# A gated linear recurrence ahead of a top-1 expert layer: every attention product 128 columns wide, and the copies, squares and limiter in another order

## The chip, the cores and the metric

The kernel runs on one core of a Trainium2 chip. The metric is the device time of one execution in microseconds (us). Five engines matter: TensorE (PE, matrix products; its weight loads are PEld), VectorE (DVE), ScalarE (ACT), GpSimd (POOL) and SyncE (SP, which issues the DMAs). Each works through its own queue in order.

## The reference

Attention is a recurrence with a complex gate per channel; the real part of its state answers the query. An expert layer follows: each token goes to the expert with its largest logit.

```python
mag = np.sqrt(a_re * a_re + a_im * a_im)
scale = np.minimum(mag, 0.999) / (mag + 1e-06)
a_re_n, a_im_n = (a_re * scale, a_im * scale)
for t in range(S):
    new_re = ar * S_re - ai * S_im
    new_im = ar * S_im + ai * S_re
    kv = np.einsum('bhd,bhe->bhde', k[:, :, t], v[:, :, t])
    S_re, S_im = (new_re + kv, new_im)
    y[:, :, t] = np.einsum('bhd,bhde->bhe', q[:, :, t], S_re)
...
expert_idx = np.argmax(logits, axis=1)
...
    h = np.maximum(xe @ w1[e], 0.0)
    ye = h @ w2[e]
    out[mask] = gate_w[mask, None] * ye
```

Sizes: batch 4, 8 heads, 768 tokens, 48 channels a head (384 in all); 8 experts with 1024 hidden units; all in 32-bit floats.

## The kernel before

The kernel has three parts: attention, routing, experts. Only attention is touched by the change.

**Preparation, per batch, on VectorE and ScalarE (`limit`, `front`).** The channels lie on partitions, in 3 tiles of 128; the 768 tokens of a batch are 6 chunks of 128 tokens, each in 8 blocks of 16 steps. `limit` works on a quarter of the steps at a time (four pieces): ScalarE squares the gates (`sq`), VectorE adds the squares (`s`), ScalarE takes logarithm, exponential and a square (`l`, `u`), VectorE and ScalarE make the scale (`sc`). `front` scales the gates of a batch (`X<-raw`, four operations), issues the loads of the next batch's gates (`raw`) and of this batch's `q` and `k` (`qt`, `kt_in`), and multiplies the gates up over 15 steps (`z`, `X<-z`). Between these steps it calls the pieces of the next batch's limiter. Then it carries the products over blocks (`carry`, `zc`). Per tile of 128 channels, `fix` applies the carry and `fold` multiplies the products into `q` and their inverse into `k` (`pk`), and sends both by DMA to the heads' tiles `KX` and `QX` (a ring of six each).

**Products (`attention`).** Heads go in three groups (2, 3 and 3 heads). For each chunk TensorE makes the scores (`at`, 224 columns: 128 of scores and 96 that move the state on), VectorE masks them (`am`), ScalarE copies the other 96 columns to `kt`. Then come the output (`y` from masked scores and values, and from the state `st`) and the next state (`sp`, copied to `st` by ScalarE); each of these products has 48 columns, one head's values. ScalarE copies `y` to `xf`. In the last group each chunk is also transposed (`px`, copied to `xt`) and multiplied with the gate weights to logits (`lg`); VectorE copies a batch's logits to `lg_all`.

**Order.** VectorE, ScalarE and TensorE run in the order in which the code is written (`InOrder`). `front` is a generator that yields estimated VectorE microseconds; `attention` is one that yields estimated TensorE microseconds. `heads_until` interleaves them: a piece of attention is emitted when the sum of VectorE estimates (`spent[0]`) has passed the sum of its own (`spent[1]`). A group is put in line 4 us (`SHIP`) after the fold that completes its heads. So a mask stands in VectorE's queue where the estimates put it; if TensorE lags, VectorE stops there, with the next batch's preparation behind.

SyncE issues all of this part's DMAs from one queue. A tile with several buffers (`bufs`) lets a load go out while earlier contents are still read; otherwise the load waits at the head of SyncE's queue, and the `KX` and `QX` copies wait behind it.

## Time and profile before

| | |
|---|---|
| median of three runs | 971.62 us (952.6 to 973.02) |
| profiled execution | 963.26 us, of it 961.5 us from first to last instruction |
| mean granted clock of TensorE | 0.806 |
| TensorE busy | 718.4 us (75%), weight loads 624.0 us |
| VectorE busy | 421.7 us (44%) |
| ScalarE busy | 208.3 us (22%) |

Busy shares are means over parts with different limits: attention ends at 566.6 us, routing at about 600, and the experts take the rest. They are best read by stretches. The granted clock is given as a share of 2.4 GHz; it has two levels, 0.50 (1.2 GHz) and 1.00 (2.4 GHz), so a value between is a mean over time. In the trace a 32-bit product is two records (`x2`). The start of one instruction to the start of the next on TensorE tells its pace; the length of a record also holds the time through the array.

### The profile page before, as it was taken

How to read it: one execution, taken by the hardware profiler on the slowest of the kernel's cores; microseconds unless marked ns; L12 is line 12 of the kernel's file. 1: busy time of each engine (PE TensorE's matmuls, PEld its weight loads, DVE VectorE, ACT ScalarE, POOL GpSimd, SP SyncE). 2: the span in 40 equal slices, each digit the busy share in tenths (PEclk: the TensorE clock that was granted, in tenths of full speed). 3: DMA queues.
4: the chain of work that ended last, by engine and by line, in shares of the span. 5: the costliest groups of instructions: out<-in, count | busy, mean ns of one | idle time of the engine just before them, and what ended most of it. 6: DMA issues, size and time to landing. Idle time of an engine off the chain costs nothing. (4 is left out here: it accounts for less than half of the span.)

```text
span 961.5 us, 10708 instructions
## 1 busy us (share of the span) xinstructions
PE 718.4 (75%) x3985; PEld 624.0 (65%) x3985; DVE 421.7 (44%) x764; ACT 208.3 (22%) x486; POOL 138.0 (14%) x160
## 2 busy tenths in 40 slices
PE   0000578893967947998499951999999999999997
PEld 0000578783967846987499840777777777777775
DVE  3779966549657568854952015111111111111111
ACT  5442343322344123322232110000000000000000
POOL 6000000000000000000000002133333333333320
PEclk9999985555577557875569555999999999999999
DMA  7301471124270134412431003878797779878860
GB/s 213 99 0 49 113 177 62 44 57 124 53 212 18 49 89 117 124 51 61 120 72 37 26 19 102 355 313 311 296 361 295 301 296 395 313 308 316 326 232 1
DMA packets 67627, 156.47 MB, mean 163 GB/s; under 512 B 9873, under 2 KB 50866, under 8 KB 59634
## 3 DMA queue, kind: packets, MB, share of 16 engines
q0 software_dynamic: 12896, 108.36, 29.3%
q1 hardware_dynamic: 51474, 47.36, 18.7%
q8 instruction: 33, 0.54, 0.2%
q10 hardware_dynamic: 3200, 0.01, 0.2%
q14 instruction: 24, 0.20, 0.1%
HBM read 127.23 MB, written 10.83 MB: 144 GB/s over the span
## 5 line engine op out<-in xcount | busy, mean ns | idle before, releaser
L57 PE MATMUL at<-QX,KX 128*128 128x224 f32 (+1 forms) x384 | 124.7, 485 | 153.6 <-DVE QX L57 137.4
L57 PEld LDWEIGHTS at<-QX,KX 128*128 128x128 f32 x384 | 95.4, 277 | 160.4 <-issue 104.4
L675 PEld LDWEIGHTS h_ps<-xt,w1t 128*128 128x128 f32 x1488 | 173.2, 194 | 13.2 <-issue 5.3
L675 PE MATMUL h_ps<-xt,w1t 128*128 128x128 f32 x1488 | 173.4, 277 | 4.9 <-issue 4.9
L681 PE MATMUL o_ps<-w2t,ht 128*128 128x384 f32 x496 | 167.8, 492 | 8.5 <-ACT ht L677 8.2
L681 PEld LDWEIGHTS o_ps<-w2t,ht 128*128 128x128 f32 x496 | 91.7, 190 | 71.7 <-ACT ht L677 14.1
L57 PE MATMUL y<-vb,am 128*128 128x48 f32 x384 | 90.6, 336 | 17.8 <-DVE am L57 15.8
L57 PEld LDWEIGHTS y<-vb,am 128*128 128x128 f32 x384 | 86.4, 270 | 21.2 <-issue 17.1
L677 ACT ACTIVATE ht<-h_ps 128x512 f32<-128x512 f32 x31 | 18.5, 597 | 357.3 <-PE h_ps L675 357.3
L57 PE MATMUL y<-st,QX 128*128 128x48 f32 x320 | 85.1, 358 | 3.0 <-ACT st L57 2.9
L683 DVE TENSOR_SCALAR yo<-o_ps,xs 128x384 f32<-128x384 f32 x31 | 19.1, 618 | 143.8 <-PE o_ps L681 143.8
L57 DVE TENSOR_TENSOR am<-at,causal 128x256 f32<-128x256 f32 x120 | 41.3, 366 | 93.1 <-ACT kt L57 70.1
L445 POOL MEMSET state<- 128x1152 f32 x1 | 1.1, 1062 | 550.1 <-PE lg L57 550.1
L670 DVE COPY xt<-xt_ps 128x384 f32<-128x384 f32 x31 | 17.3, 557 | 139.9 <-PE xt_ps L668 139.8
L57 PE MATMUL sp<-vb,kt 128*128 128x48 f32 x320 | 74.9, 334 | 0.0
L57 PEld LDWEIGHTS y<-st,QX 128*128 128x128 f32 x320 | 71.3, 275 | 4.4 <-ACT st L57 3.9
L57 PE MATMUL sp<-st,QX 128*128 128x48 f32 x256 | 64.6, 343 | 0.0
L57 PEld LDWEIGHTS sp<-vb,kt 128*128 128x128 f32 x320 | 63.5, 252 | 0.0
L684 POOL DMA_INDIRECT out_dram<-yo,idx x31 | 31.5, 1016 | 194.8 <-DVE yo L683 193.9
L57 PEld LDWEIGHTS sp<-st,QX 128*128 128x128 f32 x256 | 54.2, 261 | 0.0
L57 DVE SCALAR_TENSOR_TENSOR s<-sq 128x576 f32<-128x576 f32 (+1 forms) x28 | 23.6, 842 | 65.9 <-ACT sq L57 65.9
L57 PEld LDWEIGHTS lg<-wgate,xt 128*128 128x128 f32 x144 | 29.4, 297 | 30.0 <-ACT xt L57 30.0
(142 smaller groups left out, 757.4 us busy)
## 6 DMA issues: line engine op xcount, KB each, us to landing
KX<-pk SPq DMA_DIRECT2D x48, 146.2 KB, 3.4
QX<-pk SPq DMA_DIRECT2D x48, 144.0 KB, 3.5
raw<-in_a_re_dram SPq DMA_DIRECT2D x16, 288.0 KB, 4.9
raw<-in_a_im_dram SPq DMA_DIRECT2D x16, 288.0 KB, 5.4
qt<-in_q_dram SPq DMA_DIRECT2D x12, 384.0 KB, 5.8
kt_in<-in_k_dram SPq DMA_DIRECT2D x12, 384.0 KB, 5.8
vb<-in_v_dram SPq DMA_DIRECT2D x24, 192.0 KB, 3.0
x_hbm<-xf SPq DMA_DIRECT2D x24, 192.0 KB, 2.7
```

The lines of the kernel that those rows point to most:

```text
L57: return lambda *a, **kw: self.tc.keep_in_program_order(f(*a, **kw))
L445: nc.gpsimd.memset(state, 0.0)
L670: nc.vector.tensor_copy(xt, xt_ps)
L675: nc.tensor.matmul(h_ps[:, f, :], lhsT=w1t[:, c:c + 128], rhs=xt[:, d, :], start=(d == 0), stop=(d == DT - 1))
L677: nc.scalar.activation(ht[:, 0:FT // 2, :], h_ps[:, 0:FT // 2, :], func=ACT.Relu)
L681: nc.tensor.matmul(o_ps, lhsT=ht[:, f, :], rhs=w2t[:, f * DM:f * DM + DM], start=(f == 0), stop=(f == FT - 1))
L683: nc.vector.tensor_scalar_mul(y, o_ps, xs[:, DM:W])
L684: nc.gpsimd.indirect_dma_start(out=out[:, :], out_offset=bass.IndirectOffsetOnAxis(ap=idx[:, j:j + 1], axis=0), in_=y, in_offset=None, bou ...
```

## The change

- Every `y` and `sp` product takes 128 columns of the values: the head's own 48 and its neighbours' (`first`, `own`). PSUM tiles `y`, `sp` and the state `st` are 128 wide per head; the copy to `xf` picks the head's 48 columns, in one instruction for the first two groups and in three for the last.
- The mask of chunk c+1 is emitted ahead of the outputs of chunk c. The copies out of PSUM are emitted after the estimate for their products, and `kt` is copied after the mask.
- The logits of a chunk are emitted after the next chunk's outputs, and ScalarE instead of VectorE copies a batch's logits.
- In `limit` the squares of a piece are issued one piece ahead, into a double buffer; the order of the stages within a piece changes. In `front` the limiter is called only from step 7 on, twice a step.
- The set-up tiles of the masks lie in a pool that is freed, and `qt` and `kt_in` have one buffer instead of two.
- The estimates in the yields change.

```diff
--- before.py
+++ after.py
@@ -87,31 +87,32 @@
-    tok_i = consts.tile([128, 128], I32, name="tok_i")
...
+    with tc.tile_pool(name="setup", bufs=1) as setup:
+        tok_i = setup.tile([128, 128], I32, name="tok_i")
+        nc.gpsimd.iota(tok_i, pattern=[[1, BL], [BL, NB]], base=0, channel_multiplier=0)
...
@@ -164,12 +165,18 @@
 
         def limit(b, raws, scales):
 
-            held = {}
+            held, sqs = {}, {}
+
+            def squares(i):
+                if i < BL // JQ:
+                    sq = two.tile([128, BL, 2, C * NB], FP32, name="sq").rearrange("p j u n -> p (j u n)")[:, 0:JQ * 2 * NC]
+                    sqs[i] = sq.rearrange("p (j u n) -> p j u n", u=2, n=NC)
+                    A.activation(sqs[i], raws[i], func=ACT.Square)
+            squares(0)
             for i in range(BL // JQ + 2):
                 if i < BL // JQ:
-                    sq = one.tile([128, JQ, 2, NC], FP32, name="sq")
-                    A.activation(sq, raws[i], func=ACT.Square)
                     s = two.tile([128, JQ, NC], FP32, name="s")
+                    sq = sqs.pop(i)
                     vstt(s, sq[:, :, 0, :], 1e-12, sq[:, :, 1, :], ALU.max, ALU.add)
                     yield
                 if i >= 2:
@@ -178,14 +185,6 @@
                     sc = two.tile([128, JQ, NC], FP32, name="sc", bufs=BL // JQ)
                     vstt(sc, l, -2 / 0.999, u, ALU.max, ALU.mult)
                     scales.append(sc)
-                    yield
-                if 1 <= i <= BL // JQ:
-
-                    s1, l, u = held[i - 1]
-                    vtt(s1, s1, u, ALU.mult)
-                    yield
-                    vstt(l, s1, -3.0, l, ALU.add, ALU.mult)
-                    A.activation(u, l, func=ACT.Identity, scale=-0.5e-6 * 0.4995, bias=w_bias)
                     yield
                 if i < BL // JQ:
                     l, u = (two.tile([128, JQ, NC], FP32, name=x) for x in "lu")
@@ -193,6 +192,15 @@
                     A.activation(l, l, func=ACT.Exp, scale=-0.5)
                     A.activation(u, l, func=ACT.Square, accum_out=good[:, b, G * C + i:G * C + i + 1])
                     held[i] = s, l, u
+                    squares(i + 1)
+                if 1 <= i <= BL // JQ:
+
+                    s1, l, u = held[i - 1]
+                    vtt(s1, s1, u, ALU.mult)
+                    yield
+                    vstt(l, s1, -3.0, l, ALU.add, ALU.mult)
+                    A.activation(u, l, func=ACT.Identity, scale=-0.5e-6 * 0.4995, bias=w_bias)
+                    yield
 
         def front(b, raws, scales, heads, ahead):
 
@@ -206,18 +214,19 @@
             qs, ks = [], []
             for t in range(G):
                 for x, src in ((qs, q), (ks, k)):
-                    x.append(ld.tile([128, BL, C * NB], FP32, name="qt" if x is qs else "kt_in"))
+                    x.append(ld.tile([128, BL, C * NB], FP32, name="qt" if x is qs else "kt_in", bufs=1))
                     nc.sync.dma_start(x[t], src[b, :, t])
 
             for j in range(1, BL):
                 cur, prev = X[:, j], X[:, j - 1]
                 z = two.tile([128, 2, 2, NC], FP32, name="z")
                 vtt(z, dims(cur, 0, (NC, 2), (NC, 2), (1, NC)), dims(prev, 2 * NC, (-NC, 2), (0, 2), (1, NC)), ALU.mult)
-                next(more, None)
+                if j > 6:
+                    next(more, None)
                 vtt(cur[:, 1:3, :], z[:, 0], z[:, 1], ALU.add)
-                if j > 8:
+                if j > 6:
                     next(more, None)
-                yield 1.8
+                yield 2.4 if j > 6 else 1.3
             for _ in more:
                 pass
 
@@ -253,7 +262,7 @@
 
             def fold(t):
                 ts = slice(t * TC, t * TC + TC)
-                sq = one.tile([128, BL, 2, TC], FP32, name="sq")
+                sq = two.tile([128, BL, 2, TC], FP32, name="sq")
                 s, l = (two.tile([128, BL, TC], FP32, name=x) for x in "sl")
                 A.activation(sq, X[:, :, 1:3, ts], func=ACT.Square)
                 qp = two.tile([128, 2, KW], FP32, name="pk", bufs=3)
@@ -326,6 +335,10 @@
                 lgs[:] = [psL.tile([128, C, E], FP32, name="lg")]
             pairs = [range(p, min(p + 2, n)) for p in range(0, n, 2)]
 
+
+            first = [min(h * D, DM - 128) for h in hs]
+            own = [slice(h * D - f, h * D - f + D) for h, f in zip(hs, first)]
+
             def scores(c):
                 wide = 128 + (R2 if c < C - 1 else 0)
                 ats = []
@@ -334,17 +347,17 @@
                     for i in r:
                         T.matmul(at[:, i % 2, 0:wide], lhsT=KX[i][:, c * 128:c * 128 + 128], rhs=QX[i][:, c, 0:wide],
                                  start=True, stop=True)
-                    if c < C - 1:
-                        A.copy(KTs[c % 2][:, r[0]:r[-1] + 1, 0:R2], at[:, 0:len(r), 128:wide])
                     ats.append(at)
                 return ats
 
-            def masks(ats):
+            def masks(c, ats):
                 am = []
                 for r, at in zip(pairs, ats):
                     a = sm.tile([128, 2, 128], FP32, name="am", bufs=4)
                     vtt(a[:, 0:len(r), :], at[:, 0:len(r), 0:128], bc(causal[:, None, :], [128, len(r), 128]), ALU.mult)
                     am += [a[:, i % 2, :] for i in r]
+                    if c < C - 1:
+                        A.copy(KTs[c % 2][:, r[0]:r[-1] + 1, 0:R2], at[:, 0:len(r), 128:128 + R2])
                 spent[0] += 0.07 * len(pairs) + 0.134 * n
                 return am
 
@@ -354,47 +367,63 @@
                 vtt(QX[i][0:R2, 0:C - 1, 128:128 + R2].rearrange("p c (w d) -> p c w d", w=2),
                     bc(diag[:, None, :, :], shape), bc(ends, shape), ALU.mult)
                 spent[0] += 0.57
+            yield 0.6
             ats = scores(0)
-            yield 0.45 * n + 1.0
-            am = masks(ats)
-            st = None
+            yield 0.4 * n + 0.3
+            am = masks(0, ats)
+            st, late = None, None
+
+            def logits(c, xt):
+                for d in range(DT):
+                    T.matmul(lgs[0][:, c, :], lhsT=xt[:, d, :], rhs=wgate[:, d * E:d * E + E], start=(d == 0), stop=(d == DT - 1))
             for c in range(C):
                 if c < C - 1:
                     ats = scores(c + 1)
-                    yield 0.43 * n
-                y = psY.tile([128, 3, D], FP32, name="y")
+                    yield 0.38 * n
+                    am1 = masks(c + 1, ats)
+                y = psY.tile([128, 3, 128], FP32, name="y")
                 for i, h in enumerate(hs):
-                    T.matmul(y[:, i, :], lhsT=am[i], rhs=values[c][:, h, :], start=True, stop=(c == 0))
+                    vals = values[c].rearrange("p h e -> p (h e)")[:, first[i]:first[i] + 128]
+                    T.matmul(y[:, i, :], lhsT=am[i], rhs=vals, start=True, stop=(c == 0))
                     if c > 0:
                         T.matmul(y[:, i, :], lhsT=QX[i][:, c, 0:128], rhs=st[:, i, :], start=False, stop=True)
-                A.activation(xf[:, c, hs[0] * D:hs[-1] * D + D].rearrange("p (h e) -> p h e", e=D), y[:, 0:n, :],
-                             func=ACT.Copy, scale=-1.0)
-                yield 0.44 * n
+                if late:
+                    logits(*late)
+                    late = None
+                yield 0.46 * n
+                if own[0] == own[n - 1]:
+                    A.activation(xf[:, c, hs[0] * D:hs[-1] * D + D].rearrange("p (h e) -> p h e", e=D), y[:, 0:n, own[0]],
+                                 func=ACT.Copy, scale=-1.0)
+                else:
+                    for i, h in enumerate(hs):
+                        A.activation(xf[:, c, h * D:h * D + D], y[:, i, own[i]], func=ACT.Copy, scale=-1.0)
                 if c < C - 1:
-                    am = masks(ats)
-                    sp = psS.tile([128, 3, D], FP32, name="sp")
+                    sp = psS.tile([128, 3, 128], FP32, name="sp")
                     for i, h in enumerate(hs):
+                        vals = values[c].rearrange("p h e -> p (h e)")[:, first[i]:first[i] + 128]
                         if c > 0:
                             T.matmul(sp[:, i, :], lhsT=QX[i][:, c, 128:], rhs=st[:, i, :], start=True, stop=False)
-                        T.matmul(sp[:, i, :], lhsT=KTs[c % 2][:, i, :], rhs=values[c][:, h, :], start=(c == 0), stop=True)
-                    st = sm.tile([128, 3, D], FP32, name="st", bufs=2)
+                        T.matmul(sp[:, i, :], lhsT=KTs[c % 2][:, i, :], rhs=vals, start=(c == 0), stop=True)
+                    yield 0.46 * n
+                    st = sm.tile([128, 3, 128], FP32, name="st", bufs=2)
                     A.copy(st[:, 0:n, :], sp[:, 0:n, :])
-                    yield 0.44 * n
+                    am = am1
                 if g == G - 1:
                     px = psX.tile([128, DT, 128], FP32, name="px")
                     for d in range(DT):
                         T.transpose(px[:, d, :], xf[:, c, d * 128:d * 128 + 128], ident)
+                    yield 0.35
                     xt = sm.tile([128, DT, 128], FP32, name="xt", bufs=2)
                     A.copy(xt, px)
                     r0 = b * S + c * 128
                     nc.sync.dma_start(x_hbm[r0:r0 + 128, 0:DM].rearrange("(n j) w -> j n w", j=BL), xf[:, c, :])
-                    yield 0.5
-                    for d in range(DT):
-                        T.matmul(lgs[0][:, c, :], lhsT=xt[:, d, :], rhs=wgate[:, d * E:d * E + E], start=(d == 0), stop=(d == DT - 1))
-                    yield 0.6
+                    late = c, xt
+            if late:
+                logits(*late)
+                yield 0.7
             taken.difference_update(slots)
             if g == G - 1:
-                V.tensor_copy(lg_all[:, b * C:(b + 1) * C, :], lgs[0])
+                A.copy(lg_all[:, b * C:(b + 1) * C, :], lgs[0])
 
 
         values, lgs, spent, waiting = [], [], [0.0, 0.0], []
```

The order on three queues shows what the code makes of it.

TensorE, a chunk of the last group of batch 0. `y`, `sp`, `px` and `lg` are outputs, state, transposes and logits; `x3` is three alike. Before:

```order
L57 MATMUL y<-vb,am 128x48
L57 MATMUL y<-st,QX_133 128x48
L57 MATMUL sp<-st,QX_137 128x48
L57 MATMUL sp<-vb,kt_139 128x48
L57 MATMUL sp<-st,QX_132 128x48
L57 MATMUL sp<-vb,kt_139 128x48
L57 MATMUL sp<-st,QX_133 128x48
L57 MATMUL sp<-vb,kt_139 128x48
L57 MATMUL px<-ident,xf 128x128 x3
L57 MATMUL lg<-wgate,xt 128x8 x3
L57 MATMUL at<-QX_137,KX_131 128x224
```

The same place of the change, from the same output on:

```order
L57 MATMUL y<-vb,am 128x128
L57 MATMUL y<-st,QX_137 128x128
L57 MATMUL lg<-wgate,xt 128x8 x3
L57 MATMUL sp<-st,QX_141 128x128
L57 MATMUL sp<-vb,kt_143 128x128
L57 MATMUL sp<-st,QX_136 128x128
L57 MATMUL sp<-vb,kt_143 128x128
L57 MATMUL sp<-st,QX_137 128x128
L57 MATMUL sp<-vb,kt_143 128x128
L57 MATMUL px<-ident,xf 128x128 x3
L57 MATMUL at<-QX_141,KX_135 128x224
```

The columns go from 48 to 128, and the logits, before behind this chunk's transposes, now stand ahead of the state products and belong to the chunk before.

VectorE, masks of batch 0's attention (`am`) within the scan of batch 1 (`z`, `X`) and the limiter (`s<-sq`), with what each waits for. Before:

```order
L57 TENSOR_TENSOR am<-at,causal 128x256 [waits Activation_49]
L57 TENSOR_TENSOR am<-at,causal 128x128 [waits Activation_49]
L57 TENSOR_TENSOR z<-X 128x576 [waits DVE_49]
L57 SCALAR_TENSOR_TENSOR s<-sq 128x576 [waits Activation_49]
L57 TENSOR_TENSOR X<-z 128x288 [waits DVE_49]
L57 TENSOR_TENSOR z<-X 128x576 [waits DVE_49]
L57 SCALAR_TENSOR_TENSOR s<-sq 128x576 [waits Activation_49]
L57 TENSOR_TENSOR X<-z 128x288 [waits DVE_49]
```

The change, at the first step from which the limiter is called:

```order
L57 TENSOR_TENSOR am<-at,causal 128x256 [waits PE_49]
L57 TENSOR_TENSOR am<-at,causal 128x128 [waits PE_49]
L57 TENSOR_TENSOR z<-X 128x576 [waits DVE_49]
L57 SCALAR_TENSOR_TENSOR s<-sq 128x576 [waits Activation_49]
L57 TENSOR_TENSOR X<-z 128x288 [waits DVE_49]
L57 SCALAR_TENSOR_TENSOR s<-sq 128x576 [waits Activation_49]
L57 TENSOR_TENSOR z<-X 128x576 [waits DVE_49]
L57 TENSOR_TENSOR s<-s,u 128x576
L57 TENSOR_TENSOR X<-z 128x288 [waits DVE_49]
```

The masks waited for ScalarE (its `kt` copy) and now wait for TensorE. The two sums `s<-sq` stood a step apart and are now parted by one short operation.

SyncE, the copies of the first fold of batch 0 to the heads' tiles (`KX` of heads 0, 1 and 2), with the loads of `k` and `q` between. Before:

```order
L210 DMA kt_in<-in_k_dram 128x768 [waits DMAHW3_49,DVE_49]
L302 DMA KX_126<-pk 48x780 [waits DMAHW4_49,DVE_49,Activation_49]
L302 DMA KX_126<-pk 48x780 [waits DMAHW5_49,DVE_49,Activation_49]
L302 DMA KX_127<-pk 48x780 [waits DMAHW6_49]
L302 DMA KX_127<-pk 48x780 [waits DMAHW7_49]
L302 DMA KX_128<-pk 32x780 [waits DMAHW0_49]
L302 DMA KX_128<-pk 32x780 [waits DMAHW1_49]
```

The change:

```order
L218 DMA kt_in<-in_k_dram 128x768 [waits DMAHW1_49,DVE_49]
L311 DMA KX_130<-pk 48x780 [waits DMAHW2_49,DVE_49,Activation_49]
L311 DMA KX_130<-pk 48x780 [waits DMAHW3_49,DVE_49,Activation_49]
L311 DMA KX_131<-pk 48x780 [waits DMAHW4_49]
L218 DMA qt<-in_q_dram 128x768 [waits DMAHW5_49,DVE_49]
L311 DMA KX_131<-pk 48x780 [waits DMAHW6_49]
L311 DMA KX_132<-pk 32x780 [waits DMAHW7_49]
L311 DMA KX_132<-pk 32x780 [waits DMAHW0_49]
```

The load of the third `qt`, which waits for VectorE to have read the second, now stands between the two copies of head 1. Before, with two buffers, it went out ahead of all these copies.

## Rows read from the trace of the kernel before

**Rows 1.** Busy time per stretch: start:end length, engines' busy us (x instructions), PEclk, DMA share, GB/s.

```profile
0.00:33.50 33.50, 0.00 (x0) 0.00 (x0) 14.30 (x29) 16.93 (x25) 15.52 (x29) 1.00 0.53 153
33.50:127.25 93.75, 20.58 (x115) 19.06 (x116) 78.31 (x124) 33.52 (x67) 0.00 (x0) 0.97 0.28 71
127.25:262.33 135.08, 103.32 (x477) 97.68 (x476) 86.01 (x150) 46.48 (x115) 0.00 (x0) 0.58 0.33 88
262.33:390.18 127.85, 93.84 (x467) 87.75 (x466) 85.89 (x150) 45.61 (x112) 0.00 (x0) 0.63 0.35 93
390.18:465.00 74.82, 59.84 (x356) 56.72 (x355) 51.20 (x96) 21.63 (x62) 0.00 (x0) 0.71 0.32 87
465.00:566.60 101.60, 92.21 (x470) 87.39 (x470) 34.21 (x64) 23.98 (x73) 0.00 (x0) 0.63 0.23 55
...
600.30:961.50 361.20, 345.71 (x2074) 273.23 (x2074) 54.71 (x92) 18.51 (x31) 113.78 (x118) 0.99 0.77 295
```

**Rows 2.** Waits of the whole span: engine, line, awaited: us, times, longest.

```profile
DVE am L57 <- ACT kt L57: 70.1, 41, 9.2
DVE s L57 <- ACT sq L57: 65.9, 21, 6.0
...
DVE lg_all L57 <- PE lg L57: 38.7, 4, 13.2
...
PEld lg L57 <- ACT xt L57: 30.0, 24, 3.8
```

**Rows 3.** Busy time of two neighbouring stretches late in attention.

```profile
480.00:500.00 20.00, 19.84 (x79) 19.00 (x80) 11.33 (x18) 6.41 (x19) 0.00 (x0) 0.50 0.25 55
500.00:520.00 20.00, 19.80 (x157) 19.68 (x157) 5.51 (x16) 5.94 (x21) 0.00 (x0) 1.00 0.31 65
```

**Rows 4.** Busy time as the expert part begins.

```profile
600.00:604.00 4.00, 3.01 (x14) 3.04 (x15) 0.00 (x0) 0.00 (x0) 1.52 (x2) 0.50 1.01 427
...
608.00:612.00 4.00, 3.64 (x19) 2.48 (x18) 1.15 (x2) 0.60 (x1) 0.00 (x0) 1.00 1.01 408
```

**Rows 5.** Order of time, TensorE, clock 1.00: start, length, engine, operation.

```profile
501.65 1.37 PE L57 MATMUL at<-QX,KX 128*128 128x224 f32 x6
...
505.47 1.37 PE L57 MATMUL at<-QX,KX 128*128 128x224 f32 x6
...
507.05 0.39 PE L57 MATMUL y<-vb,am 128*128 128x48 f32 x2
507.27 0.39 PE L57 MATMUL y<-st,QX 128*128 128x48 f32 x2
```

**Rows 6.** Order of time, TensorE, one expert tile, clock 1.00.

```profile
649.18 5.52 PE L675 MATMUL h_ps<-xt,w1t 128*128 128x128 f32 x48
654.53 0.49 PE L668 MATMUL xt_ps<-ident,xs 128*128 128x128 f32 x3
```

**Rows 7.** Order of time, TensorE, clock 0.50.

```profile
545.22 0.63 PE L57 MATMUL y<-vb,am 128*128 128x48 f32 x2
545.64 0.63 PE L57 MATMUL y<-st,QX 128*128 128x48 f32 x2
...
551.42 1.63 PE L57 MATMUL at<-QX,KX 128*128 128x128 f32 x6
552.84 0.50 PE L57 MATMUL y<-vb,am 128*128 128x48 f32 x2
```

**Rows 8.** Groups by operation and shape: xcount | busy us, mean ns | idle before.

```profile
L57 ACT COPY xt<-px 128x384 f32<-128x384 f32 x24 | 11.5, 477 | 7.9 <-PE px L57 7.6
```

**Rows 9.** Order of time, SyncE and VectorE, at the start.

```profile
1.28 0.42 SPq L160 DMA_DIRECT2D raw<-in_a_re_dram  x1
...
7.87 1.01 DVE L93 CAST tok_f<-tok_i 128x128 f32<-128x128 int32 x1
...
10.01 0.25 DVE L72 TENSOR_TENSOR diag<-diag,diag 96x96 f32<-96x96 f32 x1
```

**Rows 10.** Order of time, VectorE, second fold of batch 0.

```profile
101.17 0.95 DVE L57 TENSOR_TENSOR pk<-X,qt 128x768 f32<-128x768 f32 x1
```

More of the change, by code (lines that the diff above doesn't have):

```diff
@@ L98, in gateloop_then_moe @@
-    nc.vector.tensor_scalar(out=pos_i[:, 1:2], in0=pos_i[:, 1:2], scalar1=3, scalar2=None, op0=ALU.logical_shift_right)
-    pos_f = consts.tile([128, 2], FP32, name="pos_f")
-    nc.vector.tensor_copy(pos_f, pos_i[:, 0:2])
     row = consts.tile([128, 1], FP32, name="row")
-    tt(row, pos_f[:, 0:1], pos_f[:, 1:2], ALU.add)
     causal = consts.tile([128, 128], FP32, name="causal")
-    nc.vector.tensor_scalar(out=causal, in0=tok_f, scalar1=row, scalar2=None, op0=ALU.is_ge)
-    diag_i = consts.tile([R2, R2], I32, name="diag_i")
@@ L106, in gateloop_then_moe @@
-    nc.gpsimd.iota(diag_i, pattern=[[0, 2], [1, D]], base=0, channel_multiplier=-1)
     diag = consts.tile([R2, 2, D], FP32, name="diag")
-    diag_f = consts.tile([R2, R2], FP32, name="diag_f")
-    diag_2 = consts.tile([R2, R2], FP32, name="diag_2")
-    nc.vector.tensor_copy(diag_f, diag_i)
-    flat = diag.rearrange("p u e -> p (u e)")
-    nc.vector.tensor_scalar(out=flat, in0=diag_f, scalar1=0.0, scalar2=None, op0=ALU.is_equal)
-    nc.vector.tensor_scalar(out=diag_2, in0=diag_f, scalar1=float(-D), scalar2=None, op0=ALU.is_equal)
@@ L114, in gateloop_then_moe @@
-    tt(flat, flat, diag_2, ALU.add)
+    with tc.tile_pool(name="setup", bufs=1) as setup:
+        tok_i = setup.tile([128, 128], I32, name="tok_i")
+        nc.gpsimd.iota(tok_i, pattern=[[1, BL], [BL, NB]], base=0, channel_multiplier=0)
+        tok_f = setup.tile([128, 128], FP32, name="tok_f")
+        nc.vector.tensor_copy(tok_f, tok_i)
+        pos_i = setup.tile([128, 3], I32, name="pos_i")
+        nc.gpsimd.iota(pos_i, pattern=[[0, 3]], base=0, channel_multiplier=1)
+        nc.vector.tensor_scalar(out=pos_i[:, 0:1], in0=pos_i[:, 0:1], scalar1=NB - 1, scalar2=4,
+                                op0=ALU.bitwise_and, op1=ALU.logical_shift_left)
+        nc.vector.tensor_scalar(out=pos_i[:, 1:2], in0=pos_i[:, 1:2], scalar1=3, scalar2=None, op0=ALU.logical_shift_right)
+        pos_f = setup.tile([128, 2], FP32, name="pos_f")
+        nc.vector.tensor_copy(pos_f, pos_i[:, 0:2])
+        tt(row, pos_f[:, 0:1], pos_f[:, 1:2], ALU.add)
+        nc.vector.tensor_scalar(out=causal, in0=tok_f, scalar1=row, scalar2=None, op0=ALU.is_ge)
+        diag_i = setup.tile([R2, R2], I32, name="diag_i")
+        nc.gpsimd.iota(diag_i, pattern=[[0, 2], [1, D]], base=0, channel_multiplier=-1)
+        diag_f = setup.tile([R2, R2], FP32, name="diag_f")
+        diag_2 = setup.tile([R2, R2], FP32, name="diag_2")
+        nc.vector.tensor_copy(diag_f, diag_i)
+        flat = diag.rearrange("p u e -> p (u e)")
+        nc.vector.tensor_scalar(out=flat, in0=diag_f, scalar1=0.0, scalar2=None, op0=ALU.is_equal)
+        nc.vector.tensor_scalar(out=diag_2, in0=diag_f, scalar1=float(-D), scalar2=None, op0=ALU.is_equal)
+        tt(flat, flat, diag_2, ALU.add)
@@ L181, in limit @@
                     yield
+                if i < BL // JQ:
+                    l, u = (two.tile([128, JQ, NC], FP32, name=x) for x in "lu")
+                    A.activation(l, s, func=ACT.Ln)
+                    A.activation(l, l, func=ACT.Exp, scale=-0.5)
+                    A.activation(u, l, func=ACT.Square, accum_out=good[:, b, G * C + i:G * C + i + 1])
+                    held[i] = s, l, u
+                    squares(i + 1)
                 if 1 <= i <= BL // JQ:
@@ L189, in limit @@
                     yield
-                if i < BL // JQ:
-                    l, u = (two.tile([128, JQ, NC], FP32, name=x) for x in "lu")
-                    A.activation(l, s, func=ACT.Ln)
-                    A.activation(l, l, func=ACT.Exp, scale=-0.5)
-                    A.activation(u, l, func=ACT.Square, accum_out=good[:, b, G * C + i:G * C + i + 1])
-                    held[i] = s, l, u
         def front(b, raws, scales, heads, ahead):
```

7 lines of the change are left out of this document (removed).

## Prediction

> **What bounds the kernel now.** I first cut the span at the events that the program order gives: the first scaling operation (`X<-raw`) of each batch, the end of the last batch's first `fold`, the end of attention. The busy times of the engines in these stretches [rows 1] show where the time is: attention with its preparation takes 566.6 us, the expert part from 600.3 on takes 361 us with TensorE busy for 346 of it. Nothing in the diff touches what stands behind 566.6, so only the first part can move.
>
> In the stretches of batches 1 and 2 VectorE is busy 86 of 135 and 86 of 128 us, TensorE 103 and 94. Neither is full, and neither can be taken alone: VectorE's queue holds the recurrence of the next batch and the masks of this one, in order, and stands still when a mask waits. The totals of the waits [rows 2] name what it stands for: 70.1 us for masks behind ScalarE's `kt` copy, which itself waits for TensorE's scores; 65.9 us for `s` behind the squares on ScalarE; 38.7 us for the logits' last product. All three wait, at one or two removes, for TensorE. In the last stretch (465 to 566.6) VectorE has 34 us of work and TensorE 92: there TensorE alone is the bound.
>
> Why TensorE is slow is in the granted clock. It is 0.58 to 0.71 in these stretches against 0.99 in the expert part [rows 1]. Of two neighbouring stretches with the same mix of products, both over 98% busy, one ran at 0.50 and got 79 records done, the other at 1.00 and got 157 [rows 3]. 0.50 is the level 1.2 GHz, 1.00 is 2.4 GHz. So idle time does not explain the low level here: the engine was busy throughout. What differs from the expert part is the width of the products: 128 or 384 columns there, 48 for twelve of the fifteen products of a chunk of three heads here. At the start of the expert part the clock is 0.50 from 600 to 604 and 1.00 from 608 on, after a few us of wide products behind each other [rows 4].
>
> **Edit 1, 128 columns instead of 48.** It concerns 640 products (`y` 192+160, `sp` 160+128), each two records. At the full clock a 48-wide product follows its neighbour after 507.27-507.05 = 0.22 us [rows 5]. The 24 products of 128 columns of an expert tile take 654.53-649.18 = 5.35 us, 0.223 each [rows 6]. So at 2.4 GHz the widening costs nothing: the weight load of 128 columns sets the spacing in both. At the low clock it is 545.64-545.22 = 0.42 against (552.84-551.42)/3 = 0.47 [rows 7], so 0.05 x 640 = 32 us of TensorE work if all ran there, some 22 us at today's shares.
> The Trainium skill ("TensorE: Matmul & The Clock Gate", section "Back-to-back issue gap") speaks against this edit: a product alone is spaced by its columns, N/2.4 ns and a little. By it 80 columns more on 1280 records would cost an estimated 43 us at full clock. Rows 5 and 6 do not agree with that for this stream, where each product also loads weights; the section itself says that both set the pace in such a stream.
> The gain is the clock: I forecast that stretches with all products 128 wide or wider run at 2.4 GHz a few us after they begin, as in [rows 4], and fall back only in the idle time between batches. A chunk of three heads then takes 505.47-501.65 = 3.82 us [rows 5], 1.27 per head. A cold start per batch remains: some 6 us at half pace is 3 us lost, with what queues behind it 4.
> The wider `st` copies (384 instead of 144 elements, 60 of them, 0.48 each by the `xt` copy of the same size [rows 8]) and the three `xf` copies of the last group fall on ScalarE, which is busy a third of the time; between `sp` and the next use of `st` TensorE has the next scores (1.2 us) to do. Cost 0; if ScalarE is late, 0.2 us a chunk.
>
> **Edit 2, masks before the `kt` copies, logits a chunk later, the logits' copy on ScalarE.** The mask then waits for TensorE alone; what stood in ScalarE's queue ahead of `kt` no longer holds VectorE. The 30.0 us in which TensorE waited for `xt` [rows 2] go, since the next scores and `y` stand between. The 38.7 us of VectorE for the logits move to ScalarE, where the squares of the next fold queue behind, at most 1 or 2 us a batch. Against it: the mask of chunk c+1 is now due ahead of `y` of chunk c, so VectorE has less slack when TensorE lags. In the third group TensorE needs 3.82, about 0.5 for the transposes and about 0.7 for the logits (three products at 0.22), 5.0 in all, where the pacing in the code gives it 3x1.30+0.35 = 4.25: 0.75 x 6 = 4.5 us of lag per batch that VectorE now feels.
>
> **Edit 3, limiting.** Squares are issued a step ahead, and the limiter starts at step 7 with two pieces a step. The 65.9 us shrink, but not to 0: at step 7 `s` follows the first square at once, and the second `s` stands 0.5 us behind while ScalarE has three activations and a square to do. I take 4 us left per batch, bounds 2 and 12 (ScalarE also serves attention there).
>
> **Edit 4, room.** The set-up tiles are freed, and the first load now waits for the set-up on VectorE, which today runs from 7.87 to 10.26, while the load goes out at 1.28 [rows 9]. If the set-up begins within the first 2 us and takes the same 2.4, the load goes out at up to 4.4: I take +2.8 us, bounds 1 and 5. In return the first limiter tightens. Up to 33.5 ScalarE is busy for 16.9 us [rows 1] and otherwise waits for a chain through VectorE that the early square shortens; a third of the 16.6 us of idle time is 5.5, bounds 2 and 9. One buffer for `qt` and `kt_in`: the load of the third `qt` stands on SP's queue between the `KX` copies of heads 0 and 1 and waits for three operations of the second fold, 0.95 each [rows 10]. So head 1 and all behind it come 2.4 us later (bounds 0 and 3) in each batch; VectorE's `QX` operation waits for that.
>
> **The sum**, stretch by stretch: VectorE's busy time of today [rows 1] plus the stalls that I leave.
> - to the first scaling operation: 33.5 + 2.8 - 5.5 = 30.8
> - batch 0: 78.3 + 10 (limiter 5, `KX` 2.4, folds' waits on ScalarE 2.5) = 88.3
> - batches 1 and 2: 86 + 18 each (limiter 4, third group's lag 4.5, cold start 4, `KX` 2.4, folds 3) = 104 each
> - batch 3 up to its first fold: 51.2 + 10 (no limiter) = 61.2
> - from there, TensorE: copies 4, groups at 1.27 a head-chunk 15 + 22 + 22, transposes and logits 7, last chain 2, cold start 4 = 76
>
> 464 in all, against 566.6: 102 us less. The profiled execution has 963.26 us (961.5 the span), so 861. It lies 8 us under the median of the three runs and inside their spread, and I add nothing for that.
>
> **Rivals.**
> (a) Few stalls: half of the 56 us that I leave to VectorE, so 833. For it: VectorE's busy time alone is a floor far below. Against: three engines have about the same work in the second half of each scan.
> (b) New waits: ScalarE's in-order queue, with limiter and wider copies close together, and masks that feel every lag. The stalls double: 861 + 56 = 917. For it: today's idle time comes from exactly such couplings.
> (c) The clock does not follow the columns. The Trainium skill (same page, section "HAM oscillation — how this bites in real kernels") puts a falling clock down to idle gaps of TensorE between bursts. If so, widening does nothing for the clock. In time: +22 for the products, -30 for the `xt` waits, -25 or so for the logits' copy and the limiter, hence about 930. The busy stretch at 0.50 speaks against it [rows 3].
> (d) Slower: the clock falls further. If it stays at 1.2 GHz in the stretches of batches 1 to 3 where it now averages 0.6, the 640 products cost 0.47 each, up to 32 us more on TensorE [rows 7], which is the bound at the end and paces the masks; without a gain elsewhere 963 + 32 = 995. It decides if the mean there is below 0.55 and TensorE has over 110 us of work per batch. For it only that bursts paced by VectorE leave idle time between them.
>
> **How the numbers follow.** 0.63 for the forecast (835 to 890), 0.12 for (a), 0.14 for (b), 0.08 for (c), 0.03 for (d). The range 822 to 915 holds the forecast, most of (a) and nearly half of (b), some 0.78. A difference of 2% is about what a measurement of this kernel can tell from none. Faster takes all but (d) and the slow edge of (c): 0.94; the same 0.03; slower 0.03.
>
> **What would show it.** Granted clock near 0.9 in the stretches of attention; `y` and `sp` spaced by 0.22 us; no VectorE wait for the logits; the wait of `s` under 25 us in all; masks waiting for `at` some 20 to 40 us; attention over at about 464. A clock of 0.6 there makes it wrong by (c); full clock with VectorE idle over 35 us per batch makes it wrong by (b).

## The result, and the profile after

| | before | changed |
|---|---|---|
| median | 966.75 us (952.6 to 973.02) | 883.82 us (883.22 to 885.0) |
| ratio | | 0.9235, interval 0.9157 to 0.9313 |
| profiled execution | 963.26 us, span 961.5 | 885.0 us, span 883.3 |
| mean granted clock | 0.806 | 0.901 |
| attention over at | 566.6 us | 488.3 us (forecast 464) |

Faster, as forecast, and inside the range; 23 us later than the 861 of the sum. The change cut at the same events as before (answers to [rows 1]); columns as there, the six lines of attention first:

```profile
0.00:31.10 31.10, 0.00 (x0) 0.00 (x0) 15.06 (x29) 16.97 (x25) 15.46 (x29) 1.00 0.50 140
31.10:128.80 97.70, 22.49 (x122) 21.09 (x123) 78.82 (x126) 34.28 (x68) 0.00 (x0) 0.95 0.33 86
128.80:235.70 106.90, 68.96 (x473) 65.03 (x472) 86.06 (x150) 48.62 (x127) 0.00 (x0) 0.81 0.43 112
235.70:344.40 108.70, 71.17 (x473) 67.29 (x472) 86.18 (x151) 48.71 (x127) 0.00 (x0) 0.78 0.41 110
344.40:405.90 61.50, 44.39 (x350) 42.59 (x348) 50.64 (x95) 23.32 (x75) 0.00 (x0) 0.88 0.30 78
405.90:488.30 82.40, 64.94 (x470) 62.95 (x470) 33.91 (x62) 26.25 (x86) 0.00 (x0) 0.86 0.30 76
...
520.70:883.30 362.60, 346.13 (x2074) 273.61 (x2074) 54.75 (x92) 18.53 (x31) 115.43 (x119) 0.99 0.77 296
```

TensorE has the same products (473 records where it had 477 and 467) in 69 and 71 us instead of 103 and 94; VectorE's work is unchanged, 86 us. The experts (last line) take what they took. VectorE's waits in the whole span (answers to [rows 2]):

```profile
DVE am L57 <- PE at L57: 52.4, 42, 4.1
DVE s L57 <- ACT sq L57: 27.2, 15, 5.3
...
DVE pk L57 <- DMA KX<-pk: 20.6, 3, 7.0
DVE QX L57 <- DMA KX<-pk: 10.1, 4, 2.7
...
DVE pk L57 <- DMA QX<-pk: 7.1, 1, 7.1
```

The masks' wait for `kt` and the wait for the logits within the batches are gone, `s` fell from 65.9 to 27.2. (At the end of attention the first operation behind it, `least`, waits 8.4 us while TensorE makes the last logits.) New is `pk`: four waits of about 7 us, one a batch, that the kernel before did not have. The same place in batch 0 as a timeline of VectorE, ScalarE and TensorE (start, length; in brackets the idle time ahead and what ended it):

```profile
108.00 1.82 DVE L57 TENSOR_TENSOR pk<-X,l 128x768 f32<-128x768 f32 x2
116.59 0.96 DVE L57 TENSOR_TENSOR pk<-X,qt 128x768 f32<-128x768 f32 x1 [6.77 <-DMA KX<-pk]
117.46 0.42 DVE L57 TENSOR_TENSOR am<-at,causal 128x256 f32<-128x256 f32 x1
```
```profile
117.97 0.32 ACT L57 COPY kt<-at 128x192 f32<-128x192 f32 x1 [6.71 <-DVE am L57]
...
120.41 0.23 ACT L57 ACTIVATE xf<-y 128x96 f32<-128x96 f32 x1
```
```profile
120.69 0.80 PE L57 MATMUL y<-vb,am 128*128 128x128 f32 x2 [8.70 <-ACT xf L57]
```

Fold 2's queries (the third fold's) may not be written until fold 1's `KX` copies have left the buffer. A mask stands behind them on VectorE, `kt` and then `xf` behind the mask on ScalarE, and the next outputs behind `xf` on TensorE: all three engines stop. SyncE's queue (SPq) shows when the copies go out:

```profile
95.30 4.37 SPq L312 DMA_DIRECT2D QX<-pk  x6
107.77 0.33 SPq L218 DMA_DIRECT2D kt_in<-in_k_dram  x1
109.01 4.60 SPq L311 DMA_DIRECT2D KX<-pk  x7
113.65 0.65 SPq L312 DMA_DIRECT2D QX<-pk  x1
114.34 0.59 SPq L311 DMA_DIRECT2D KX<-pk  x1
114.98 5.25 SPq L312 DMA_DIRECT2D QX<-pk  x3
```

The load of the third `kt_in` stands ahead of fold 1's `KX` copies and goes out at 107.77, when VectorE has read the second `kt_in`. It does not hold these copies back: the first goes out at 109.01, as soon as VectorE has written the first half of the keys (two `pk` operations in 1.82 us from 108.00 on). Eight `KX` copies follow, 0.66 us each on the queue; the time that they take to go out and land is what fold 2's queries wait for. What the load does hold back is two of fold 1's eight `QX` copies: six went out from 95.30 on, two stand behind the load, among and behind the `KX` copies.

### The profile page after: what moved, and what is told of

The parts are those of the page before. It is cut to its first block, busy times and chain, and to the rows that moved or that the text cites. A ratio compares the mean times of both kernels' runs of the same rounds, so it can differ in the third digit from the quotient of the medians.

```text
span 883.3 us, 10745 instructions
## 1 busy us (share of the span) xinstructions
PE 621.0 (70%) x3985; PEld 534.7 (61%) x3985; DVE 422.3 (48%) x760; ACT 218.3 (25%) x538; POOL 138.0 (16%) x160
## 5 line engine op out<-in xcount | busy, mean ns | idle before, releaser
L57 PE MATMUL at<-QX,KX 128*128 128x224 f32 (+1 forms) x384 | 92.3, 382 | 165.9 <-DVE QX L57 165.9
L57 PEld LDWEIGHTS at<-QX,KX 128*128 128x128 f32 x384 | 73.4, 215 | 171.2 <-issue 98.1
L57 PE MATMUL y<-vb,am 128*128 128x128 f32 x384 | 78.3, 298 | 42.9 <-ACT xf L57 42.9
L57 PEld LDWEIGHTS y<-vb,am 128*128 128x128 f32 x384 | 67.1, 212 | 44.6 <-ACT xf L57 44.1
L57 PE MATMUL y<-st,QX 128*128 128x128 f32 x320 | 67.4, 294 | 3.4 <-ACT st L57 2.9
L57 PE MATMUL sp<-vb,kt 128*128 128x128 f32 x320 | 62.0, 288 | 0.0
L57 PEld LDWEIGHTS y<-st,QX 128*128 128x128 f32 x320 | 52.2, 205 | 6.6 <-ACT st L57 6.6
L57 PE MATMUL sp<-st,QX 128*128 128x128 f32 x256 | 52.7, 289 | 0.0
L57 ACT COPY kt<-at 128x192 f32<-128x192 f32 (+1 forms) x100 | 25.5, 288 | 102.3 <-DVE am L57 102.3
L57 DVE TENSOR_TENSOR z<-X 128x576 f32<-128x576 f32 x60 | 45.1, 752 | 0.7
```

The source lines that it names most:

```text
L57: return lambda *a, **kw: self.tc.keep_in_program_order(f(*a, **kw))
```

## Experiments

All are timed beside the kernel before, whose median in the three groups of runs was 966.5 to 967.4.

**Width: w_only and u_48.** The first is the kernel before with 128 columns in `y`, `sp` and `st`, the `xf` copies that pick 48 of them, and the freed set-up pool; the second is the changed kernel without the width. This is u_48's edit (the same for `sp` and `st`); w_only widens the same tiles in the kernel before:

```diff
-                y = psY.tile([128, 3, 128], FP32, name="y")
+                y = psY.tile([128, 3, 48], FP32, name="y")
...
-                    vals = values[c].rearrange("p h e -> p (h e)")[:, first[i]:first[i] + 128]
+                    vals = values[c].rearrange("p h e -> p (h e)")[:, first[i]:first[i] + 48]
```

> The kernel before with 128 columns alone (the set-up tiles lie in a freed pool as in the change, to make room, which costs some 3 us at the start). Theory, width moves the clock: clock in attention from 0.6 to 0.8 or more, time from 963 to about 905 us (890 to 925). Rival, the clock follows idle gaps: clock near 0.6, and the wider products cost 0.05 us each at the low level, so 985 us.

> The changed kernel with its attention products back at 48 columns (PSUM tiles and state too), all else as changed. Theory, width moves the clock: mean granted clock in attention falls from about 0.85 back to 0.6 or 0.7, masks wait longer for the scores, and the time goes from 884 to about 925 us (910 to 945). Rival, idle gaps of TensorE set the clock and the other edits closed them: clock in attention stays near 0.85 and the time within 5 us of 884.

w_only: 889.59 us, ratio 0.9185 (0.913 to 0.924), just under the 890 to 925 expected. u_48: 915.86, ratio 0.9466 (0.9406 to 0.9527), within the 910 to 945 expected. Busy times by stretch, batches 1 and 2, of w_only and then of u_48:

```profile
129.60:242.00 112.40, 72.87 (x473) 68.04 (x472) 85.47 (x151) 48.85 (x125) 0.00 (x0) 0.82 0.41 107
242.00:354.60 112.60, 72.84 (x473) 68.25 (x472) 85.48 (x151) 48.85 (x125) 0.00 (x0) 0.80 0.40 106
```
```profile
132.20:248.40 116.20, 86.02 (x472) 81.91 (x472) 86.69 (x149) 45.64 (x115) 0.00 (x0) 0.66 0.39 103
248.40:361.60 113.20, 81.61 (x474) 77.77 (x473) 86.32 (x150) 45.80 (x115) 0.00 (x0) 0.68 0.40 105
```

With the old order the width alone lifts the clock from 0.58 and 0.63 to 0.82 and 0.80 and takes 77 us off. So the clock follows the columns, and rival (c) falls. The other edits without the width give 51, and the width on top of them 32: both shorten the same waits (the masks': 93 us before, 45 in w_only, 76 in u_48, 52 in the changed kernel), and their gains don't add (77 + 51 against 83). Seen from w_only, the other edits add 6 us in the changed kernel (889.6 against 883.8), less than can be told from none, but 45 in the kernel q_pool below (844.7).

**Some of the width: u_96** (the changed kernel with `first`, `y`, `sp` and `st` at 96):

```diff
-                y = psY.tile([128, 3, 128], FP32, name="y")
+                y = psY.tile([128, 3, 96], FP32, name="y")
```

> The changed kernel with the y and sp products at 96 columns in place of 128 (48 gave 915.9). It leaves nothing out. Theory (the clock follows the columns streamed): the granted clock of the batches lies between 0.66 and 0.81 (48 and 128 columns), nearer to 128, and the time between, 888 to 900. Rival (128 is a step: below it the clock behaves as at 48): 908 to 918. Rival (96 is enough): 881 to 886.

889.79 us, ratio 0.9212 (0.9159 to 0.9266), within the 888 to 900 of the theory, an interval that overlaps that of 128 columns; granted clock 0.79 and 0.77 in batches 1 and 2, where 128 columns had 0.81 and 0.78 and 48 had 0.66 and 0.68. Between 48 and 96 columns lies nearly all of it.

**The new wait: q_pool, u_pk, q_bad, b_pool.** q_pool is the changed kernel with one word changed, so that GpSimd's queue issues the loads of `q` and `k`:

```diff
-                    nc.sync.dma_start(x[t], src[b, :, t])
+                    nc.gpsimd.dma_start(x[t], src[b, :, t])
```

> The changed kernel with the loads of q and k issued by GpSimd instead of SyncE, one buffer each as in the change. Theory, the copies to the heads' tiles stand behind these loads on SyncE's queue, and the third fold's buffer thus comes free late: the waits of VectorE for DMA before pk (7 us in each of four batches) and QX (2.4 us each) go, and with them 37 us, so about 847 us (842 to 856). Rival, the wait is for the transfers themselves (bandwidth): the waits stay and the time is 875 to 884.

844.70 us (844.19 to 845.92), ratio 0.8726 (0.8674 to 0.8779): faster than both kernels. The stretches of attention, and SyncE's queue and VectorE where batch 0 stood still:

```profile
31.30:117.60 86.30, 19.76 (x126) 18.28 (x127) 78.62 (x127) 34.23 (x68) 3.22 (x6) 1.00 0.36 95
117.60:213.90 96.30, 66.00 (x472) 61.32 (x472) 85.67 (x149) 48.20 (x127) 3.22 (x6) 0.86 0.47 124
213.90:312.40 98.50, 69.60 (x470) 65.95 (x469) 86.06 (x151) 48.55 (x127) 3.22 (x6) 0.81 0.47 121
312.40:373.80 61.40, 44.37 (x349) 42.59 (x348) 50.55 (x95) 23.26 (x75) 1.07 (x2) 0.88 0.32 81
373.80:445.90 72.10, 62.87 (x470) 60.50 (x470) 33.69 (x64) 26.00 (x86) 1.07 (x2) 0.94 0.35 88
```
```profile
93.88 5.85 SPq L312 DMA_DIRECT2D QX<-pk  x8
105.56 5.53 SPq L311 DMA_DIRECT2D KX<-pk  x8
```
```profile
106.28 0.95 DVE L57 TENSOR_TENSOR pk<-X,qt 128x768 f32<-128x768 f32 x1
```

The theory held. All eight of fold 1's `QX` copies now go out ahead of the `KX` copies. No wait of `pk` is left, and the four stretches with a third fold are each 10.2 to 11.4 us shorter.

But this edit moved two things. The three buffers of `pk` are dealt out when the program is built, and by their addresses the one word changed how. In the kernel before and in q_pool, the queries of a batch's three folds share one buffer; in the changed kernel fold 2's queries get the buffer of fold 1's keys. u_pk writes the old sequence into the changed kernel, q_bad the new one into q_pool:

```diff
-                qp = two.tile([128, 2, KW], FP32, name="pk", bufs=3)
-                kp = two.tile([128, 2, KW], FP32, name="pk", bufs=3)
+                use = ['cacbca', 'abacab', 'bcbabc', 'cacbca'][b][2 * t:2 * t + 2]
+                qp, kp = (two.tile([128, 2, KW], FP32, name="pk" + x, bufs=1) for x in use)
```

(q_bad: `'cacbba', 'acabbc', 'cacbba', 'acabbc'`.)

> The changed kernel, loads of queries and keys on SyncE as in it, but with the three pk buffers written out by hand in the sequence of the kernel before (the queries of all three folds of a batch in one buffer, the keys of fold 1 in another). It leaves nothing out. Theory (the wait for pk comes from the buffer that fold 2's queries get, which is the one that fold 1's keys are still being copied from): the 27.7 us of pk waits go and some 20 to 28 us of time with them: 855 to 865; the rest of the way to 844.7 is the queue, the KX copies standing behind kt_in (QX waits 10 us). Rival (the loads standing on SyncE's queue are the whole of it, and the buffer only shows the delay): fold 1's query copies, too, go out late, so pk waits on as much: 875 to 884.

> The other corner: loads of queries and keys issued by GpSimd (the run of 844.7), but the pk buffers written out by hand in the sequence of the changed kernel (fold 2's queries in the buffer of fold 1's keys). It leaves nothing out. Theory: with the copies not held behind loads on SyncE, fold 1's keys are out some 5 us after their last write, so fold 2's queries wait only 0 to 3 us a batch: 845 to 857. Rival (the buffer alone is the cause): the 7 us a batch come back in full: 868 to 875.

u_pk: 888.58 us, ratio 0.9202 (0.9148 to 0.9256). q_bad: 873.11, ratio 0.9035 (0.8983 to 0.9088). My theory failed for both, and each rival held (u_pk some 5 us above its bound). The wait in u_pk, and then in q_bad with its copies:

```profile
117.16 0.96 DVE L57 TENSOR_TENSOR pkc<-X,qt 128x768 f32<-128x768 f32 x1 [7.54 <-DMA QX<-pkc]
```
```profile
106.68 5.28 SPq L311 DMA_DIRECT2D KX<-pkb  x8
```
```profile
114.09 0.96 DVE L57 TENSOR_TENSOR pkb<-X,qt 128x768 f32<-128x768 f32 x1 [6.61 <-DMA KX<-pkb]
```

Either cause alone brings the wait. With the loads on SyncE, fold 1's last two query copies go out late, so the old buffer is no freer than the new one. With the loads away, the keys' eight copies still need 5.3 us of queue from the first half of the keys on, and whoever takes their buffer at once waits for them. Only with both undone is the wait gone. The 39 us fall into two parts: moving the loads, with the changed kernel's buffers kept, is worth 11 (883.8 against 873.1), and the buffers then 28 (873.1 against 844.7). In the other order the parts are not the same: the buffers alone give nothing (888.6), the loads then 44.

b_pool makes q_pool's edit in the kernel before.

> The kernel before with nothing changed but that the loads of queries and keys are issued by GpSimd. It leaves nothing out. Theory: with two buffers the loads stand on SyncE's queue only when their buffer is free, so moving them is worth nothing where nothing waits for KX: 960 to 972 (ratio 0.99 to 1.01). Rival: SyncE's queue is late in itself, and the loads' place there costs the kernel before too: 925 to 950.

967.94 us (951.37 to 976.44) beside 966.52 (960.44 to 972.63): no gain that can be told. The four runs scatter by 25 us, so a difference of a per cent or two stays open; the 925 to 950 of the rival is out. Where two buffers let the loads go out early, nothing like the 39 us is to be had from their queue.

**The order of the copies: q_kt.** q_pool with `kt` copied ahead of the masks and the masks behind the outputs, as before:

```diff
+                    if c < C - 1:
+                        A.copy(KTs[c % 2][:, r[0]:r[-1] + 1, 0:R2], at[:, 0:len(r), 128:wide])
                     ats.append(at)
...
-                    am1 = masks(c + 1, ats)
```

> The changed kernel with the loads of queries and keys issued by GpSimd (the run of 844.7), and with the order of the PSUM copies as in the kernel before: kt ahead of the masks, and the masks of step c+1 behind the y products. It leaves nothing out. Theory: masks stand behind ScalarE's kt copies again, so VectorE's wait am<-kt returns; with 128 columns alone it was 37 us against 46 us of am<-at here, so the gain of this edit was in what VectorE does not wait for between batches: 850 to 860. Rival: with 128 columns TensorE is late for the masks either way (am waits 46 us for at), so the order of the copies is worth nothing: 842 to 848.

848.79 us, ratio 0.8781 (0.8729 to 0.8833), against 0.8726 (0.8674 to 0.8779): not to be told apart, and under 1 us above the rival's 842 to 848. The theory's 850 to 860 failed. VectorE's waits for masks in this kernel:

```profile
DVE am L57 <- ACT kt L57: 38.8, 29, 4.2
...
DVE am L57 <- PE at L57: 6.7, 3, 3.5
```

45.5 us under two names, where q_pool has 46.1 under one. The name of the wait changed, its length did not, since TensorE is what both wait for.

**The logits: q_lg.** q_pool with the logits right behind their transposes, and `lg_all` copied by VectorE:

```diff
-                    late = c, xt
+                    yield 0.5
+                    logits(c, xt)
+                    yield 0.6
```

> The same kernel of 844.7 with the logits as before: each block's logits right behind its transposes and the xt copy, and the copy lg_all on VectorE. It leaves nothing out. Theory: with 128 columns alone TensorE waited 23.6 us for xt and VectorE 16.9 us for the logits; the third group's steps lie on the path that VectorE's folds wait behind, so about half comes back: 855 to 865. Rival: TensorE has slack against VectorE in batches 0 to 2 and only the last batch's six steps pay (6 x 1 us): 846 to 851.

858.57 us, ratio 0.8891 (0.8846 to 0.8935): 14 us for the two together, as the theory had it. Its waits, VectorE and TensorE:

```profile
DVE am L57 <- PE at L57: 61.1, 41, 5.1
```
```profile
PE lg L57 <- ACT xt L57: 15.0, 24, 0.7
```

TensorE waits 15 us for `xt`, the masks wait 15 us longer for TensorE.

**The limiter: u_limit and q_lim.** u_limit is the changed kernel with the limiter called from the first step on, squares still ahead; q_lim is q_pool with the whole limiter as before:

```diff
-                if j > 6:
-                    next(more, None)
+                next(more, None)
...
-                if j > 6:
+                if j > 8:
                     next(more, None)
-                yield 2.4 if j > 6 else 1.3
+                yield 1.8
```

> The changed kernel with the limiter called from the first step on, as before (one piece a step, two from step 9, 1.8 us a step in the pacing); squares still issued ahead. Theory, calling it late takes away waits for squares: VectorE's waits of s grow by 5 to 10 us in each of three batches, so 905 us (895 to 915). Rival, the squares issued ahead already do it, and late calls only crowd ScalarE: 880 to 886.

> The same kernel of 844.7 with the whole limiter as before: squares issued in their own step, the stage order of before, calls from the first scaling step on, and the price 1.8 a step. It leaves nothing out. Theory: prefetch is worth the s<-sq wait: with 128 columns alone it stood at 64.3 us against 27.2 here, and the late calls were worth 3 us by themselves; the first limiter, where nothing covers it, costs 5 us more (36.5 against 31.3), the other batches about 3 to 5 each: 855 to 865. Rival: VectorE waits elsewhere instead for TensorE (am<-at) and only the first limiter pays: 848 to 851.

u_limit: 886.71 us, ratio 0.9152 (0.9095 to 0.921): the theory's 895 to 915 failed, and the late calls are worth nothing that can be told. q_lim: 881.24, ratio 0.913 (0.9085 to 0.9174): 36.5 us, far over the 10 to 20 expected. VectorE's wait from the first scaling operation to the last batch's first fold, in q_pool and then in q_lim:

```profile
L57 DVE SCALAR_TENSOR_TENSOR s<-sq 128x576 f32<-128x576 f32 (+1 forms) x22 | 18.6, 844 | 14.5 <-ACT sq L57 14.5
```
```profile
L57 DVE SCALAR_TENSOR_TENSOR s<-sq 128x576 f32<-128x576 f32 (+1 forms) x22 | 18.6, 847 | 44.5 <-ACT sq L57 44.5
```

30 us here, and 5.2 ahead of the first scaling operation (36.5 against 31.3). Since the late calls gave nothing in the changed kernel, the early squares and the new stage order are what is left to carry the limiter's gain; no run parts these two.

**A warm start: q_warm.** q_pool with 24 more products of 128 columns at the end of each batch's fold 0, into a tile that nobody reads:

```diff
+                if t == 0:
+                    px = psX.tile([128, DT, 128], FP32, name="px")
+                    for _ in range(24):
+                        T.matmul(px[:, 0, :], lhsT=ident, rhs=kp[:, 0, 0:128], start=True, stop=True)
```

> The same kernel of 844.7 with 24 products of 128 columns more, in each batch at the end of fold 0, into a PSUM tile that nobody reads, so that TensorE does not stand idle ahead of the first group of the batch. Theory: the granted clock falls to 0.5 in the idle gap at each batch's start and the first group then runs its first products at half pace; the 24 products run at half pace in the gap and the group starts at full clock: 2 to 3 us a batch, 833 to 839. Rival: the products end later than the group could start, or the products of the first group wait for masks and folds anyway: 843 to 848.

847.47 us, ratio 0.8785 (0.8742 to 0.8827): no gain, as the rival had it. The granted clock at the last batch's start (5-us stretches):

```profile
380.00:385.00 5.00, 5.00 (x41) 4.89 (x40) 3.43 (x7) 0.49 (x2) 0.00 (x0) 1.00 0.74 202
385.00:390.00 5.00, 5.00 (x41) 4.97 (x40) 4.93 (x8) 1.47 (x7) 0.19 (x1) 1.00 0.17 37
390.00:395.00 5.00, 3.01 (x24) 2.76 (x23) 4.93 (x8) 4.05 (x11) 0.35 (x1) 1.00 0.59 155
395.00:400.00 5.00, 4.37 (x22) 4.07 (x23) 4.49 (x6) 1.43 (x5) 0.00 (x0) 0.66 0.54 128
```

The group started at full clock, but fell back to 0.66 behind the idle time of 390 to 395: in this batch the slow spell was moved rather than removed. The 24 products also cost what they gave. The group's first scores took 1.68 us where q_pool had 3.53, but they began at 382.31, when the 24 products had ended, some 2 us after VectorE's `QX` operation had freed them (from 379.62, two in 1.37 us). What the slow spell costs stays open.

## Why the prediction was right, and where it was short

| stretch | forecast | measured | q_pool |
|---|---|---|---|
| to the first scaling operation | 30.8 | 31.1 | 31.3 |
| batch 0 | 88.3 | 97.7 | 86.3 |
| batch 1 | 104 | 106.9 | 96.3 |
| batch 2 | 104 | 108.7 | 98.5 |
| batch 3 to its first fold | 61.2 | 61.5 | 61.4 |
| from there to the end | 76 | 82.4 | 72.1 |

**Edit 1 held.** 128 columns cost nothing at full clock: in the trace after, `y` and `sp` follow each other at 0.22 us, as [rows 5, 6] had it:

```profile
132.30 0.39 PE L57 MATMUL y<-st,QX 128*128 128x128 f32 x2
132.52 0.39 PE L57 MATMUL sp<-st,QX 128*128 128x128 f32 x2
132.74 0.39 PE L57 MATMUL sp<-vb,kt 128*128 128x128 f32 x2
```

TensorE's busy time in attention fell from 370 to 272 us. By the rule of the Trainium skill in "TensorE: Matmul & The Clock Gate", section "Back-to-back issue gap", taken for a product alone, the columns would have added an estimated 43 us at full clock; these rows do not agree with it for this stream.

The clock rose, though to 0.78 to 0.95 rather than 0.9 throughout. TensorE stands idle between batches, and the clock is low there, as in the same trace where batch 0 has ended:

```profile
180.00:200.00 20.00, 2.67 (x23) 2.34 (x22) 19.04 (x28) 6.57 (x17) 0.00 (x0) 0.58 0.42 114
```

TensorE busy for 2.67 of 20 us, clock 0.58. With this row the Trainium skill agrees ("TensorE: Matmul & The Clock Gate", section "HAM oscillation — how this bites in real kernels", the rule behind rival (c)): idle gaps pull the clock down. The row doesn't speak against edit 1: the low level comes with idle time, and it came with 48-wide products too, with the engine full [rows 3].

**Edit 2 held in its larger half.** No wait for logits is left in the batches. Masks wait for `at` 52 us (20 to 40 forecast), 31 of them in the last stretch, where TensorE is the bound; in batches 1 and 2 it is 4.5 and 5.6, where the sum had 4.5 for the third group's lag. Moving the logits and their copy is worth 14 us; the masks ahead of `kt`, which the prediction told first, are worth nothing that can be measured.

**Edit 3 held.** `s` waits 4.2, 4.8 and 5.1 us in batches 0 to 2 (4 to 5 taken); the whole wait is 27.2, a little over the 25 named. The first scaling operation came within 0.3 us, and not by luck: in w_only, with the freed set-up and no early squares, it starts 3.0 us later than before (2.8 taken), and the early squares and stage order are worth 5.2 there by q_lim (5.5 taken).

**Edit 4 is the step that failed.** The prediction saw that the load of `qt` waits on SyncE's queue between the `KX` copies and priced that at 2.4 us a batch, 9.6 in all. So far it was right: the `QX` operation waits 2.4 to 2.7, and moving the loads with the buffers kept (q_bad) is worth 10.7 us. It did not ask which buffer each `pk` would get. In the changed kernel fold 2's queries get that of fold 1's keys, while the eight `KX` copies still read it: 6.8 to 7.1 us of VectorE per batch, 27.7 in all. The sum had no such term, and priced only the operation that reads the copies' target, not the one that overwrites their source. Nor did it see that the load of `kt_in` holds back two `QX` copies of fold 1, so that the old buffer would have been no better (u_pk). By q_pool, one buffer on that queue together with the buffers it led to costs 42 us of attention (488.3 against 445.9), where the forecast had 9.6 (2.4 a batch).

**One term was too large, in the other direction.** 42 less 9.6 would put attention's end 33 us late, and it was 24 late. In q_pool, batch 1 and the last stretch come out 7.7 and 3.9 us under the forecast. With the terms for `KX` (2.4) and cold start (4) struck where the sum had them, the forecasts for batches 0 to 2 and the end are 85.9, 97.6, 97.6 and 72, against 86.3, 96.3, 98.5 and 72.1 measured. So the two terms account for the difference. That the cold start costs nearly nothing is only argued from this fit, since q_warm didn't take the slow spell away. It is luck that the total came out 23 us late and not 33: this term stood against the missing one.

The rivals: (a), half the stalls, is what q_pool comes near to (844.7 against 833). (b) was right in kind, a new wait in place of the old ones, but named ScalarE's queue and the masks; it was the buffers of `pk` and SyncE's queue. (c) and (d) fell with w_only.

## What to carry to other kernels

When a tile loses a buffer, follow its load through the whole queue, and for every copy that falls behind it ask both who reads its target and who next overwrites its source. Then look which buffer each rotating tile really gets: an edit elsewhere can deal them out anew, and here that was 28 us. A load that may have to wait belongs on a queue where nothing urgent stands behind it: here one word was worth 39 us, the 28 for the buffers among them, beside the 83 of the whole change. Before reordering copies for a wait, ask what both the old and the new releaser wait for; if it is the same engine, only the wait's name changes.

## What the runs showed of the hardware

- 32-bit products of 48, 96 and 128 columns, each with its weight load, follow each other at the same 0.22 us at full clock ([rows 5]; 131.86 and 132.08 in u_96's timeline; 132.30 and 132.52 above), but 48 columns left the clock of batches 1 and 2 at 0.66 and 0.68, 96 at 0.79 and 0.77, 128 at 0.81 and 0.78.
- In q_warm the products before an idle gap of 2.59 us ran at full clock, and those soon behind it at half pace, 0.42 us a product. In q_pool, behind a gap of 2.07 us at the same place, they went on at 0.22 (394.50, 394.72 in its timeline). These are single places, and no rule follows from them. q_warm:

```profile
392.17 0.39 PE L57 MATMUL sp<-vb,kt 128*128 128x128 f32 x2
...
395.60 0.49 PE L57 MATMUL y<-vb,am 128*128 128x128 f32 x2 [2.59 <-ACT xf L57]
...
396.86 0.63 PE L57 MATMUL sp<-st,QX 128*128 128x128 f32 x2
397.28 0.63 PE L57 MATMUL sp<-vb,kt 128*128 128x128 f32 x2
```

- The issue of a `KX` copy holds SyncE's queue for about 0.66 us (5.28 for eight in q_bad; a `kt_in` load takes 0.33), so eight copies that become ready together leave over 5 us, long beside the 0.95 us of the operation that waits for the last of them.
